# Moving three weight stages' conversion steps within the opening of an mLSTM and bilinear MoE kernel

## The chip, the cores and the metric

The kernel runs on one core of one Trainium2 chip. The metric is the device time of one execution in microseconds (us); the lower, the better. The core has TensorE (matrix products, PE in the profile, with its weight loads as PEld), VectorE (DVE), ScalarE (ACT), GpSimd (POOL) and SyncE (SP), which here issues the transfers between DRAM and the core's memory. Each engine works through its own instructions in order and waits for the others by semaphores.

## The reference

Two parts follow one another. The first is an mLSTM over 768 steps for 4 batches and 8 heads with a head dimension of 40; the second a bilinear layer with 1536 hidden units on all 3072 tokens, without a nonlinearity.

```python
for t in range(S):                                     # S = 768, for every batch and head
    m_new  = maximum(f_gate[t] + m, i_gate[t])
    f_stab = exp(f_gate[t] + m - m_new); i_stab = exp(i_gate[t] - m_new); m = m_new
    C = f_stab * C + i_stab * outer(v[t], k[t])        # 40 x 40 state
    n = f_stab * n + i_stab * k[t]
    y[t] = sigmoid(o_gate[t]) * (C @ q[t]) / maximum(abs(n @ q[t]), 1)
x   = y as [3072 tokens, 320]
out = ((x @ w_a) * (x @ w_b)) @ w_out                  # w_a, w_b: 320 x 1536; w_out: 1536 x 320
```

The weights arrive as 64-bit floats; everything else is 32 bits.

## The kernel before

**The mLSTM in chunks.** The sequence of each batch is cut into 6 chunks of 128 steps, so there are 24 chunks of work (n = 0 to 23, four batches to each position c). Within a chunk the recurrence becomes products of matrices: `begin_a` transposes q and k on TensorE (tile pT), `begin_e` makes the table of decays E, `begin_b` forms the scores pS and multiplies by E, `begin_c` multiplies by v (pV), `stage_u` updates the state (pU, from vw, which `weigh` makes on GpSimd), `stage_f` divides by the denominator and multiplies by the sigmoid of the output gate (the chunk's y, in tile osig), and `stage_d` transposes y on TensorE (pX) and splits it into a rounded part xh (ScalarE) and a remainder xl (VectorE). Later chunks use stages of the same names with operands of 16 bits in three parts, and pass the state through DRAM: `stage_u` rounds it into the tile cb (L648, L652, L655), writes it to c_dram (L658, L659) and reads it back (L661).

**The MoE in blocks.** The 24 chunks are grouped into 9 blocks of 2 or 3. For a block, `moe_block` runs over 12 slices of hidden units: `up` forms the products with w_a and w_b (pu, L812) from xh and xl, multiplies the two (g, L818 and L819) and splits the result (gh, gl); `down` multiplies by w_out into pd (L783).

**The weights in stages.** There are 32 weight stages; stages 0 to 7 serve the first three slices of hidden units: 0 to 3 are 128-row parts of w_a and w_b, 4 holds the last 64 rows of both, 5 to 7 are parts of w_out. Each stage is loaded as 64-bit words by `fetch` (L386, tile raw) and turned into a rounded 32-bit part and a remainder by four steps, each of which does its work once and calls the one it rests on:

- `signs(x)`: one Prelu on ScalarE (L414) takes sign and exponent from the upper words.
- `words(x)`: three operations on VectorE (L425, L426, L428) put the upper part together (tile cw) and the remainder from the lower words (tile cr).
- `leading(x)`: one rounding copy on ScalarE (L441).
- `rests(x)`: two products with plus and minus the identity on TensorE (pc, L451 and L452) and a sum on VectorE (L459) make the rounded-off remainder. For stage 4 the two 64-row halves are handled apart (L456 twice on ScalarE, L457 twice on VectorE).

`cw` and `cr` are rings of four places, `step` (written by signs) has four places too, and pc shares the three buffers of pu.

**The opening.** `start` (from L956 on) is written out by hand: `in_order` ties each engine's instructions into the order in which they stand in the text. It computes the first two chunks (n = 0 and 1), converts stages 0 to 4, and is left when both chunks' xh and xl and stage 4 are there, since the first `up` needs them. `busy(k)` issues k products of zeros (L961) that nothing reads; they occupy TensorE. `run(x, k)` advances a generator by k steps, or to its end; `run(d0, 1)` issues pX of chunk 0 and the next `run(d0)` its xh and xl. `gate_o(0, slice(0, 2))` is the sigmoid on the gates of the first two chunks (L218). The loads stand in the same function: SyncE issues them in the order q, k, weight stages, v, gates and so on, and `load(NS + 2)`, `fetch(18)`, `load(NS + 3)`, `fetch(26)` are the last ones there.

**Behind the opening.** The gates of the remaining steps are computed by `gates_rest`, again in order, which writes the decay table to DRAM (g_dram, L291); `load_g` reads a chunk's part back to all partitions (L225, tile gbc). The rest of the mLSTM, the MoE blocks and the conversion of the remaining stages are traced in one interleaved loop (the loop over kb at L1073); the order on each engine there comes from a planner, which simulates a timeline while it schedules the instructions.

Of the kernel before, what the change touches and what calls it, by code (L numbers as in the profile page):

```python
# [20 lines left out]
def kernel(  # L21
# [158 lines left out]
    def nat(n):  # L180
        return inner.get(n) or (qk[n % NQ], va[n % NQ])
# [33 lines left out]
    def gate_o(c, bs=slice(0, B)):  # L215
        hot[0] = 3
        x = osig[c][:, bs, 0:DM]
        nc.scalar.activation(x, x, AF.Sigmoid)  # L218
# [187 lines left out]
    def signs(x):  # L406
        if not turn(0, x):
            return
        raw, n = held[x]
        t = step[x % len(step)][:, :n]  # L410
        words = raw.bitcast(U32).rearrange("p (n w) -> p n w", w=2)
        held[x] += [t, words[:, :, 0]]
        with tc.issue_after(rounded[x - 2]) if x > 4 else nullcontext():
            nc.scalar.activation(  # L414
                t, words[:, :, 1].bitcast(F32), AF.Prelu, scale=2.0 ** -112, alpha=-(2.0 ** 32)
            )
# [16 lines left out]
    def leading(x):  # L433
        if not turn(2, x):
            return
        n, W, r = held[x]
        w = ws[x] = rpool.tile([P, 2, n], F32R, tag=f"s{x - 1}", name=f"w{x}")
        h = w[:, 0]
        if len(stages[x]) > 1:
            h = cpool.tile([P, WCH], F32R, tag="ct", name="ct", bufs=2)  # L440
        rounded[x] = nc.scalar.copy(h, W).ins  # L441
        held[x] += [w, h]
# [474 lines left out]
    def begin_c(n):  # L917
        c, b = chunks[n]
        s = st[n]
        if n >= NS:  # L920
            weigh(n)
        if n < NS:
            pV = ps_dn.tile([P, 512], F32, tag=f"pd{min(n, 2)}", name=f"pV{n}")
        else:
            pV = ps_at.tile([P, 512], F32, tag="pat", name=f"pV{n}")
        pv = pV[:, 0:H * DV].rearrange("p (h d) -> p h d", h=H)
        dense(n, pV, 3)
        for h in range(H):
            nc.tensor.matmul(pv[:, h], s["E"][:, h, :], nat(n)[1][:, h], start=True, stop=True)  # L929
            if h % HH == HH - 1:  # L930
                yield
        if c > 0:
            nc.vector.tensor_tensor(s["num"], pv, s["num"], op=ALU.add)
        else:
            s["num"] = pv
        yield
# [14 lines left out]
    with tc.tile_pool(name="spool", bufs=3) as spool:  # L951
# [4 lines left out]
        def start():  # L956
# [8 lines left out]
            def run(x, count=99):  # L965
                for _ in range(count):
                    if next(x, "end") == "end":
                        return
# [38 lines left out]
            rests(0)  # L1007
            run(b1)
            leading(1)
            gate_o(0, slice(0, 2))  # L1010
            rests(1)
            run(begin_c(0))
            weigh(0)
            signs(2)
            run(begin_c(1))
            run(stage_f(0))
            words(2)
            run(stage_u(0))
            load(NS + 2)
            weigh(1)  # L1020
            leading(2)
            signs(3)
            run(stage_f(1))
            d0, d1 = stage_d(0), stage_d(1)
            warm = ps_dn.tile([P, 512], F32, tag="pd2", name="warm2")
            busy(4)
            run(d0, 1)
            words(3)
            run(d0)
            leading(3)  # L1030
            busy(4)
            rests(2)
            signs(4)
            run(stage_u(1))
            fetch(18)
            load(NS + 3)
            fetch(26)
            busy(4)
            run(d1, 1)
            words(4)  # L1040
            run(d1)
            leading(4)
            busy(4)
            rests(3)
            busy(8)
            rests(4)
            signs(5)
            gate_o(0, slice(2, B))
# [71 lines left out]
```

## Time and profile before

| | us |
|---|---|
| three runs | 551.63, 552.08, 550.17 |
| median | 551.63 |
| the profiled execution | 551.88 |
| its span | 550.1 |
| TensorE busy | 537.8 (98%) |
| VectorE busy | 411.6 (75%) |
| ScalarE busy | 269.2 (49%) |
| GpSimd busy | 149.5 (27%) |

All times below are counted from the start of the span. Matmuls are pipelined, so TensorE's busy time includes time in which it does not work at its peak. A row of a timeline gives start, duration, engine, line, operation, what is written and read, a count, and, in square brackets, how long the engine had stood idle before and what ended that. A row of the chain of waits gives start, duration and what ran or was awaited. A row of the windows gives the stretch, its length, the busy time of TensorE, its weight loads, VectorE, ScalarE and GpSimd with the number of instructions, then the granted clock of TensorE (1.00 is full), the mean busy share of the 16 DMA engines and GB/s.

### The profile page before, as it was taken

To read this page: it belongs to the slowest core of one execution; us is meant where nothing else is said; L and a number is where in the kernel's file an instruction comes from. 1 tells how busy PE (TensorE), PEld (TensorE's weight loads), DVE (VectorE), ACT (ScalarE), POOL (GpSimd) and SP (SyncE) were. 2 spreads that over 40 slices of the span, in tenths; PEclk is the share of its full clock that TensorE was granted. 3 is DMA by queue.
4 is the path that set the end of the run, shared out by engine and by line. 5 is a ranking of instruction groups with operands and counts; after the bars stand their busy time and mean duration, and the time that the engine had idled before them with its cause. 6 is when DMAs were issued, how large, how long until landed. Compare 5 with 4: busy or idle time off the path is not lost.

```text
span 550.1 us, 11947 instructions
## 1 busy us (share of the span) xinstructions
PE 537.8 (98%) x4493; PEld 511.4 (93%) x4493; DVE 411.6 (75%) x906; ACT 269.2 (49%) x645; POOL 149.5 (27%) x224
## 2 busy tenths in 40 slices
PE   8999999899999999999999999999999899999997
PEld 5888888799999999999999999999999899999996
DVE  6889999977768785988868974988677846964332
ACT  5574488664425853645625664655354813321111
POOL 3102324545032340442233340444041203210000
PEclk9799999999999999999999999999999999999999
DMA  9999943284537665668646885758459403300001
GB/s 190 217 220 284 323 88 71 64 179 113 89 100 142 139 128 113 133 131 179 121 119 115 127 161 116 140 123 170 91 130 183 102 1 104 78 1 24 1 1 36
DMA packets 198549, 66.71 MB, mean 121 GB/s; under 512 B 184220, under 2 KB 191772, under 8 KB 198492
## 3 DMA queue, kind: packets, MB, share of 16 engines
q1 hardware_dynamic: 198444, 65.86, 56.6%
q8 instruction: 35, 0.57, 0.5%
q14 instruction: 22, 0.18, 0.1%
q10 hardware_dynamic: 48, 0.10, 0.0%
HBM read 41.11 MB, written 5.95 MB: 86 GB/s over the span
## 4 chain that ended last, share of the span: by engine, by line
PE 80%; DVE 6%; DMA 4%; ACT 4%; issue 2%; SPq 2%; POOL 0%; ACTq 0%; DVEq 0%; POOLq 0%
PE pu L812 42%; PE pd L783 20%; PE pU L630 3%; PE pV L603 3%; PE pS L544 3%; DMA T<-qks 2%; DMA osig<-in_o_gate_dram 1%; PE pX L709 1%; PE pV L929 1%; ACT gbc L492 1%; PE pI L570 1%; PE pS L886 1%; PE warm L961 1%; SPq L524 1%; PE pc L451 1%
## 5 line engine op out<-in xcount | busy, mean ns | idle before, releaser
L812 PE MATMUL pu<-xh,w 128*128 128x384 f32 (+1 forms) x1080 | 273.2, 322 | 1.5 <-DVE w L459 0.7
L812 PE MATMUL pu<-xl,w 128*128 128x384 f32 (+1 forms) x648 | 206.1, 320 | 0.0
L812 PEld LDWEIGHTS pu<-xh,w 128*128 128x128 f32 x1080 | 188.3, 188 | 4.0 <-DVE w L459 1.3
L783 PE MATMUL pd<-w,gh 128*128 128x320 f32 x576 | 127.2, 311 | 0.2 <-DVE gh L821 0.2
L812 PEld LDWEIGHTS pu<-xl,w 128*128 128x128 f32 x648 | 121.8, 188 | 0.0
L819 DVE TENSOR_TENSOR g<-pu,g 128x384 f32<-128x384 f32 (+1 forms) x108 | 54.4, 504 | 82.8 <-PE pu L812 47.6
L783 PEld LDWEIGHTS pd<-w,gh 128*128 128x128 f32 x576 | 96.3, 188 | 0.6 <-DVE gh L821 0.4
L818 ACT COPY g<-pu 128x384 f32<-128x384 f32 (+1 forms) x90 | 39.6, 440 | 103.3 <-PE pu L812 96.0
L783 PE MATMUL pd<-w,gl 128*128 128x320 f32 x288 | 84.7, 311 | 0.0
L614 POOL TENSOR_TENSOR num<-v,num 128x168 f32<-128x168 f32 x36 | 21.3, 593 | 210.3 <-DVE v L610 209.7
L823 DVE TENSOR_TENSOR gl<-g,gh 128x384 fp32r<-128x384 f32 (+1 forms) x92 | 57.3, 622 | 2.0
L492 ACT ACTIVATE gbc<-gbc,gtab 128x128 f32<-128x128 f32 x160 | 49.4, 390 | 12.3 <-POOL gbc L485 12.2
L783 PEld LDWEIGHTS pd<-w,gl 128*128 128x128 f32 x288 | 52.7, 188 | 0.2
L821 DVE CAST gh<-g 128x384 fp32r<-128x384 f32 (+1 forms) x108 | 42.2, 390 | 1.7
L515 ACT CAST qks<-r 128x320 bf16<-128x320 f32 x36 | 16.4, 458 | 30.1 <-DVE r L514 30.0
L610 DVE TENSOR_REDUCE v<-pV 128x168 f32<-128x504 f32 x36 | 24.1, 675 | 9.2 <-PE pV L603 9.1
L485 POOL TENSOR_SCALAR_AFFINE_SELECT gbc<-gbc 128x1024 f32<-128x1024 f32 x20 | 23.4, 1171 | 24.7 <-DMA gbc<-g_dram 23.3
L584 POOL TENSOR_TENSOR vw<-va,gtab 128x336 f32<-128x336 f32 x20 | 17.0, 852 | 47.5 <-PE pU L630 22.2
L553 DVE TENSOR_TENSOR gbc<-gbc,pb 128x512 f32<-128x512 f32 x36 | 25.4, 707 | 4.5 <-ACT pb L551 4.5
L520 ACT COPY qks<-qks 128x640 bf16<-128x640 bf16 x36 | 26.1, 725 | 0.7
L549 DVE TENSOR_TENSOR gbc<-pS,gbc 128x512 f32<-128x512 f32 x36 | 24.3, 679 | 1.7 <-PE pS L544 1.7
L551 ACT CAST pb<-gbc 128x512 bf16<-128x512 f32 x36 | 22.2, 617 | 5.7 <-DVE gbc L549 5.6
(152 smaller groups left out, 810.1 us busy)
## 6 DMA issues: line engine op xcount, KB each, us to landing
gbc<-g_dram SPq DMA_DIRECT2D x20, 512.0 KB
q<-in_q_dram SPq DMA_DIRECT2D x24, 160.0 KB
k<-in_k_dram SPq DMA_DIRECT2D x24, 160.0 KB
va<-in_v_dram SPq DMA_DIRECT2D x24, 160.0 KB
osig<-in_o_gate_dram SPq DMA_DIRECT2D x24, 160.0 KB
raw<-in_moe_w_out_dram SPq DMA_DIRECT2D x12, 320.0 KB
out_dram<-o SPq DMA_DIRECT2D x24, 160.0 KB
raw<-in_moe_w_a_dram SPq DMA_DIRECT2D x8, 384.0 KB
```

The lines of the kernel that those rows point to most:

```text
L485: nc.gpsimd.affine_select(E, E, pattern=[[0, H], [1, P]], compare_op=ALU.is_ge, fill=-1e30, base=0, channel_multiplier=-1,)
L492: nc.scalar.activation(E[:, h], E[:, h], AF.Exp, bias=beta[:, h:h + 1])
L520: nc.scalar.copy(qks[:, 0, :, lo:lo + 2 * D], qks[:, 1, :, D - lo:3 * D - lo])
L549: nc.vector.tensor_tensor(E, pS, E, op=ALU.mult)
L553: nc.vector.tensor_tensor(E, E, pb[:, 0], op=ALU.subtract)
L610: nc.vector.tensor_reduce(t, pv.rearrange("p h i d -> p h d i"), axis=mybir.AxisListType.X, op=ALU.add)
L783: nc.tensor.matmul(pd[t][:, 0:DM], a[:, cols], w, start=(ff == 0 and first), stop=(ff == NF - 1 and last),)
L812: nc.tensor.matmul(acc[j], a, r, start=(x == 0), stop=(x == len(terms) - 1),)
L818: (nc.vector.tensor_copy if ff in [1, 2] else nc.scalar.copy)(g, acc[0])
L819: nc.vector.tensor_tensor(g, acc[1], g, op=ALU.mult)
L821: nc.vector.tensor_copy(gh, g)
L823: (nc.gpsimd if kb * 12 + ff < 16 else nc.vector).tensor_tensor(gl, g, gh.bitcast(F32), op=ALU.subtract)
```

## The change

In `start` the steps of stages 2, 3 and 4 are put elsewhere among the chunks' steps. The signs of stage 2 stand in front of the sigmoid `gate_o` and its words between the two chunks' `begin_c`; its leading part and the signs of stage 3 stand ahead of the first chunk's y (`stage_f(0)`), the words of stage 3 right after it, and `rests(2)` in front of the first transpose. The second chunk's y (`stage_f(1)`) moves behind the first transpose, the leading part of stage 3 and the signs of stage 4; the words of stage 4 and `rests(3)` follow it. The second transpose stands ahead of a group of zero products and not behind it. One group of four and one group of eight zero products are gone, which the diff counts as twelve; the description of the change speaks of sixteen. The loads keep their order.

```diff
             run(b1)
             leading(1)
+            signs(2)
             gate_o(0, slice(0, 2))
             rests(1)
             run(begin_c(0))
             weigh(0)
-            signs(2)
+            words(2)
             run(begin_c(1))
+            leading(2)
+            signs(3)
             run(stage_f(0))
-            words(2)
+            words(3)
             run(stage_u(0))
             load(NS + 2)
             weigh(1)
-            leading(2)
-            signs(3)
-            run(stage_f(1))
+            rests(2)
             d0, d1 = stage_d(0), stage_d(1)
             warm = ps_dn.tile([P, 512], F32, tag="pd2", name="warm2")
-            busy(4)
             run(d0, 1)
-            words(3)
             run(d0)
             leading(3)
+            signs(4)
+            run(stage_f(1))
             busy(4)
-            rests(2)
-            signs(4)
+            words(4)
+            rests(3)
             run(stage_u(1))
             fetch(18)
             load(NS + 3)
             fetch(26)
+            run(d1, 1)
             busy(4)
-            run(d1, 1)
-            words(4)
+            leading(4)
             run(d1)
-            leading(4)
             busy(4)
-            rests(3)
-            busy(8)
             rests(4)
             signs(5)
             gate_o(0, slice(2, B))
```

## The prediction

> **What bounds the kernel now.** I read the page first, for the span and the load of the DMA engines.
>
> ```profile
> span 550.1 us, 11947 instructions
> ...
> DMA  9999943284537665668646885758459403300001
> ```
>
> The profiled execution took 551.88 us for its span of 550.1 us, so 1.78 us lie outside the span; the median of the three runs is 551.63, which is 0.25 us below the profiled one. A change in the span is subtracted from 551.88 and the result lowered by 0.25 to stand beside the median. The DMA row has its first five slices, up to about 69 us, at 9: the opening and the first MoE block lie under a saturated DMA.
>
> The second view is the chain of waits from 19 to 31 us, the stretch in which the change lies. Columns are start, duration and what ran.
>
> ```profile
> 19.49 1.47 PE pU L630 x16
> ...
> 22.20 0.64 PE pX L709 x3
> 22.84 1.12 PE warm L961 x4
> 23.96 0.32 PE pc L451
> 24.28 0.32 PE pc L452
> 24.60 1.16 PE pU L630 x16
> ...
> 26.43 0.33 PE pX L709 x3
> ...
> 27.68 1.16 PE warm L961 x8
> ```
>
> All of it is TensorE, in the order written out by hand: the first chunk's pU ends at 20.96, the first transpose pX waits behind four zero products until 22.20, the rounding products pc of stage 2 come at 23.96, the second pX at 26.43. The rows also show two speeds: three transposes take 0.64 us at 22.20 and 0.33 at 26.43. The windows say why (the number after the engines' busy times is the granted TensorE clock, then the DMA share):
>
> ```profile
> 18.44:19.00 0.56, 0.56 (x5) 0.56 (x4) 0.48 (x2) 0.24 (x1) 0.00 (x0) 0.50 1.52 141
> ...
> 25.26:25.35 0.09, 0.09 (x8) 0.09 (x6) 0.09 (x1) 0.00 (x0) 0.00 (x0) 0.96 1.10 400
> ```
>
> The clock is at half from 18.44 to 25.26.
>
> Third, VectorE's and ScalarE's rows of the same stretch.
>
> ```profile
> 17.30 0.17 DVE L671 TENSOR_SCALAR den<-pV 128x8 f32<-128x8 f32 x1 [0.36 <-PE pV L929]
> ...
> 18.52 0.49 DVE L682 TENSOR_TENSOR osig<-y,osig 128x320 f32<-128x320 f32 x1
> 18.93 0.35 DVE L425 TENSOR_SCALAR cw<-qks 128x384 uint32<-128x384 uint32 x1
> ...
> 19.71 0.56 DVE L428 SCALAR_TENSOR_TENSOR cr<-raw,qks 128x384 fp32r<-128x384 uint32 x1
> 20.19 0.16 DVE L671 TENSOR_SCALAR den<-pV 128x8 f32<-128x8 f32 x1
> ...
> 21.35 0.85 DVE L682 TENSOR_TENSOR osig<-y,osig 128x320 f32<-128x320 f32 x1
> ...
> 23.46 0.55 DVE L714 TENSOR_TENSOR xl<-pX,xh 128x384 fp32r<-128x384 f32 x1
> 24.63 0.56 DVE L459 TENSOR_TENSOR w<-pc,cw 128x384 fp32r<-128x384 f32 x1 [0.62 <-PE pc L452]
> ...
> 27.31 0.56 DVE L714 TENSOR_TENSOR xl<-pX,xh 128x384 fp32r<-128x384 f32 x1 [0.86 <-ACT xh L713]
> ...
> 29.66 1.14 DVE L457 TENSOR_TENSOR w<-pc,cw 64x384 fp32r<-64x384 f32 x2 [1.33 <-PE pc L452]
> ```
>
> ```profile
> 16.20 1.28 ACT L218 ACT_TABLE_LOAD   x1 [1.90 <-DMA osig<-in_o_gate_dram]
> ...
> 18.14 0.54 ACT L414 ACTIVATE qks<-raw 128x384 f32<-128x384 f32 x1
> ...
> 21.61 0.56 ACT L414 ACTIVATE qks<-raw 128x384 f32<-128x384 f32 x1
> 22.23 0.25 ACT L683 COPY osig<-osig 128x64 f32<-128x64 f32 x1
> ...
> 23.66 0.55 ACT L414 ACTIVATE qks<-raw 128x384 f32<-128x384 f32 x1
> ```
>
> VectorE is the engine that stands idle while TensorE works off its order: 0.62 us before 24.63, 0.86 before 27.31, 1.33 before 29.66. The opening's last weight step that the MoE needs, L457 of stage 4, ends at 29.66 + 1.14 = 30.80.
>
> Last, what follows the opening, by windows and then around the one long wait of the first block.
>
> ```profile
> 37.00:54.00 17.00, 17.00 (x147) 15.10 (x145) 16.90 (x44) 7.45 (x18) 3.73 (x5) 1.00 1.02 260
> ...
> 71.00:77.00 6.00, 5.83 (x46) 5.36 (x46) 6.00 (x16) 6.00 (x20) 1.17 (x2) 1.00 0.02 5
> 77.00:110.00 33.00, 30.98 (x232) 27.69 (x231) 32.36 (x82) 24.45 (x59) 14.20 (x20) 1.00 0.40 78
> ```
>
> ```profile
> 54.29 0.34 SPq L291 DMA_DIRECT2D g_dram<-va  x1
> ...
> 62.23 0.33 SPq L225 DMA_DIRECT2D gbc<-g_dram  x1
> 62.67 0.69 SPq L658 DMA_DIRECT2D c_dram<-cb  x2
> 63.90 0.68 SPq L659 DMA_DIRECT2D c_dram<-cb  x2
> ```
>
> ```profile
> SPq L225 <- DMA g_dram<-va: 3.3, 1, 3.3
> ```
>
> ```profile
> 63.20 0.76 POOL vw L584
> ...
> 64.24 3.65 DMA c_dram<-cb
> ```
>
> ```profile
> 68.04 0.33 ACT L648 CAST cb<-cst 128x168 bf16<-128x168 f32 x1 [3.81 <-DMA c_dram<-cb]
> ```
>
> ```profile
> 67.47 1.32 POOL L485 TENSOR_SCALAR_AFFINE_SELECT gbc<-gbc 128x1024 f32<-128x1024 f32 x1 [2.38 <-DMA gbc<-g_dram]
> ```
>
> ```profile
> 69.52 0.42 DVE L819 TENSOR_TENSOR g<-pu,g 128x256 f32<-128x256 f32 x1 [1.68 <-ACT g L818]
> ```
>
> From 37 to 54 us VectorE is busy 16.90 of 17 and from 77 to 110 us 32.36 of 33, so time that VectorE wins in the opening is worth as much up to the next meeting point. That point is at 62 to 69 us. SyncE waits 3.3 us at L225 until the gate table has been written to DRAM (issued at 54.29, landed when L225 goes at 62.23); only then do the state's writes L658 and L659 follow in its queue; the last of them lands at 64.24 + 3.65 = 67.89; ScalarE has sat for 3.81 us at L648, which needs that buffer, and all behind it on ScalarE (a leading part L441, signs L414, the copy g L818) waits too. VectorE then runs dry for 1.68 us. The gate table's read also ends late: GpSimd begins with it at 67.47.
>
> **The change part by part.** *Signs of stage 2 ahead of the sigmoid.* One Prelu of 0.54 us goes ahead of a ScalarE instruction that stood idle for 1.90 us until its gate landed (row 16.20). If the weights have landed by about 15.6, the idle time covers it and it costs nothing; without that cover it is 0.54 us on the sigmoid. The row at 18.14 has no idle time, so they landed by 18.14 at the latest; I take covered.
>
> *Words of stage 2 ahead of the first y.* The three VectorE operations run from 18.93 to 19.71 + 0.56 = 20.27, 1.34 us, and now stand in front of the y that ran from 17.30 to 18.52 + 0.49 = 19.01. So the first y ends about 1.3 us later, near 20.3, and with its copy of 0.25 us (row 22.23) near 20.6. Its reader pX cannot start before TensorE is through pU (20.96) and, now, the products pc of stage 2. That cover holds with 1.0 us to spare (21.60 below).
>
> *TensorE's order.* After pU come pc of stage 2 (0.32 + 0.32 at half clock, to 21.60), pX (0.64, to 22.24), four zero products (1.12, to 23.4), pc of stage 3 (0.64, to 24.0), pU of the second chunk (1.16, to 25.2). ScalarE's rounding and VectorE's xl follow pX by 23.46 - 22.84 = 0.62, so xl runs from 22.86 to 23.41. *The second y* then takes what it took from 20.19 to 21.35 + 0.85 = 22.20, 2.0 us, or the first one's 1.7: it ends at 25.1 to 25.4, with the copy at 25.4 to 25.7. So pX of the second chunk starts there against 26.43: 0.7 to 1.0 us won, and TensorE waits for it 0.2 to 0.5 us, a wait that the kernel before did not have; behind it stand only the zero products and pc of stage 4.
>
> *VectorE to the end of the opening.* Words of stage 4 (1.34), the difference of stage 3 (0.55), xl (0.56) and L457 of stage 4 (1.14) now run back to back: 25.1 to 25.4 + 3.6 = 28.7 to 29.0. The last pc does not hold them up: pX 0.33, eight zero products 1.16 (the row at 27.68), pc 0.35 give 27.5. Against 30.80 the opening ends **1.8 to 2.1 us earlier; I take 2.0**.
>
> *The zero products.* The diff drops one group of four and one of eight: twelve, where the description says sixteen. At full clock eight cost 1.16 us. The dropped ones lay on the chain, and their price is inside the 2.0, not beside it.
>
> *Bounds of the opening.* Signs of stages 3 and 4 move ahead of the y copies on ScalarE. The rows at 21.61 and 23.66 have no idle time, so the weights landed by then; signs of stage 4 come near 23.3 in the new order, which costs nothing that matters. Signs of stage 3 come near 18.7; had its weights landed only at 21.61, the first y copy would end at 21.61 + 0.54 + 0.25 = 22.4, pX 0.8 later than above, and the gain would be 1.2. I take about 2.0: 18.7 is 18.14, where ScalarE was through the sigmoid, plus a rounding of half a microsecond, and nothing on ScalarE waited for weights after the gate's wait that ended at 16.20. The leading parts (L441), moved with them, run on ScalarE in time that it has: its next use, the copy of the first y, does not come before 20.3; the copy of the second y stands behind the leading part of stage 3 and the signs of stage 4, which end near 23.9, 1.2 us before that y. The DMA issues keep their order on SyncE; nothing moves past another there.
>
> *What is late next.* In the rows of 62 to 69 us the DMA's dates do not move: its share is 1.02 from 37 to 54 us and it is full until the row 71 to 77 shows 0.02, so bytes that are issued in the same order land at the same time. L225 still goes at 62.23 and L658 at 62.67 to 63.36. The write L659 at 63.90 followed a GpSimd product (63.20 + 0.76) that would now be done 2 us sooner, so it can start at 63.36, 0.54 earlier. The gate table's read ends at 67.47 as before. ScalarE therefore comes to L648 two microseconds early and waits about 5.3 us instead of 3.81; VectorE's idle 1.68 becomes about 3.1. Of the 2.0 us, **between 0 and 0.6 come through; I take 0.5**, as the chain names that product as the releaser of the write.
>
> Sum: 551.88 - 0.5 = 551.4 in the profiled execution's own time, 551.1 beside the median.
>
> The Trainium skill, page "TensorE: Matmul & The Clock Gate", section "Part 1: The HAM clock gate (the "warmup" mystery)", says that the clock is halved after an idle activity window of about 3.4 us and restored after a busy one, and that the windows run free. The trace agrees: 25.26 - 18.44 = 6.82 us is two such windows. The rule speaks against taking zero products away; by it the gate could open later than in my sum, and that is the rival on the clock below.
>
> **The rivals.** *The gain is kept.* The order behind the opening is made by a planner that simulates time, and not by hand. If the table's write (54.29) goes out ahead of two of the weight loads, or other work is laid in front of L648, the meeting at 68 us moves along and all 2.0 us come through: 549.6 (549.0 to 550.4). For it: VectorE is full from 77 to 110 us, so nothing after the meeting gives the time back. Against it: table and loads that it competes with become ready by steps that all move earlier together.
>
> *The planner turns it to a loss.* L648 is placed further ahead on ScalarE, since the plan starts 2 us earlier, and the work that ran before 64.24 now stands behind a wait that ends at 67.9 whatever is done. Place: ScalarE at L648. Price: what is pushed behind the wait, at most the 2.0 us, then VectorE starts its full stretch with that much undone: 551.63 + 2.0 = 553.6. It decides once over half a microsecond of rounding work has changed sides, as that is all the nearer meeting gives. Against it: at 64.24 three short operations stood behind L648, and the plan put them there for reasons that move together.
>
> *The clock stays low.* If the lighter order leaves the gate shut until 25.26 + 3.41 = 28.67, the second pX and eight zero products take 0.64 + 2.32 instead of 0.33 + 1.16, L457 ends near 30.4, and 0.4 of the 2.0 is left; the meeting hides it: 551.4. One more 3.41 us, to 32.1, would cost the MoE's first 2.8 us 1.4 more, putting GpSimd's product at 63.20 some 1.2 later and the end at 552.9. For it: twelve zero products fewer. Against it: from 21.85 to 25.26 the same four zero products, pX and pc run as before, and more of pU.
>
> *The opening is no earlier.* A wait for weights that the rows do not show eats the 2.0: 551.6.
>
> **How the numbers follow.** Forecast (opening 2.0 earlier, 0 to 0.6 through): 0.48. Gain kept: 0.27. Planner's loss: 0.12. Clock: 0.08. No earlier: 0.05. What this kernel's measurement can tell from no change is about 0.3%, 1.65 us, so faster is below 549.98 and slower above 553.28. Faster: three quarters of the kept gain (0.20) and 0.05 of the forecast through a plan that differs a little, 0.25. Slower: more than half of the planner's loss and a fifth of the clock's, with 0.02 for the rest, 0.11. The range runs from 548.9, the kept gain's low end, to 553.3, short of the planner's full loss. The likeliest case alone spans 550.4 to 551.9.
>
> **What would show it.** Right: pc of stage 2 directly behind pU and the second pX near 25.5; L457 ending near 28.8; L225 again near 62.2 and ScalarE's wait at L648 over 5 us, ending near 67.5. The forecast is wrong if the wait at L648 ends before 66.5 or is gone, if the half clock lasts beyond 25.3, or if L225 goes before 61. A second y that ends after 26 would refute the walk through VectorE.

## The result and the profile after

The changed kernel takes 555.54 us (median of 13 runs, 552.45 to 560.42) against 552.08 us for the kernel before in the same comparison (median of 13). The ratio is **1.0072, with a 95% interval from 1.0044 to 1.0100**: slower, by 2.4 to 5.5 us. The prediction was 551.1 us, its range ended at 553.3, and it gave slower a chance of 0.11. It was wrong. Four of the 13 runs had a granted clock of 0.984 to 0.986 and took 559.1 to 560.4 us, the profiled execution (559.08) among them, and the other nine had 0.992 or more and took 552.5 to 557.7, with a median of 554.69 that is still 2.6 us above the kernel before.

The page of the changed kernel, its span and the granted clock of TensorE in 40 slices of 13.9 us:

```profile
span 557.3 us, 11927 instructions
...
PEclk9999996899999999999999999999999999999999
```

Half clock lay at 18.44 to 25.26 us before; that slice, the second, is full here. In its place the seventh and the eighth, 84 to 111 us, have 0.6 and 0.8.

The opening, in the timelines of TensorE, VectorE and ScalarE:

```profile
19.00 0.92 PE L630 MATMUL pU<-vw,k 128*64 128x42 f32 x16
19.86 0.45 PE L451 MATMUL pc<-cr,eye 128*128 128x384 f32 x1
...
24.26 0.52 PE L709 MATMUL pX<-ident,osig 128*128 128x128 f32 x3 [1.12 <-DVE osig L682]
```

```profile
27.08 0.56 DVE L714 TENSOR_TENSOR xl<-pX,xh 128x384 fp32r<-128x384 f32 x1
...
27.90 1.14 DVE L457 TENSOR_TENSOR w<-pc,cw 64x384 fp32r<-64x384 f32 x2
```

```profile
26.19 0.50 ACT L414 ACTIVATE qks<-raw 128x320 f32<-128x320 f32 x1 [1.18 <-DMA raw<-in_moe_w_out_dram]
26.59 0.46 ACT L713 CAST xh<-pX 128x384 fp32r<-128x384 f32 x1
```

The products pc of stage 2 follow pU directly, and L457 ends at 27.90 + 1.14 = 29.04, inside the 28.7 to 29.0 that were forecast to 0.04 us and 1.76 earlier than the 30.80 of before. The second pX comes at 24.26, not at 25.5, because this execution had the full clock in the opening. What it won there it lost again at a wait that the prediction did not have: the signs of stage 5 on ScalarE wait 1.18 us for a weight load, the second chunk's rounding xh stands behind them, and xl and L457 follow. In the text of `start` these signs come behind `run(d1)`, which issues xh, and behind `rests(4)`; ScalarE's order in this opening was therefore not that of the text, which the prediction walked through. Why is not known.

The meeting at 62 to 69 us, the rows that answer to those of before (SyncE's queue, ScalarE, GpSimd, VectorE):

```profile
61.48 0.33 SPq L225 DMA_DIRECT2D gbc<-g_dram  x1
```

```profile
67.80 0.33 ACT L648 CAST cb<-cst 128x168 bf16<-128x168 f32 x1 [2.18 <-DMA c_dram<-cb]
```

```profile
67.16 1.09 POOL L485 TENSOR_SCALAR_AFFINE_SELECT gbc<-gbc 128x1024 f32<-128x1024 f32 x1 [3.82 <-DMA gbc<-g_dram]
```

```profile
68.44 0.42 DVE L819 TENSOR_TENSOR g<-pu,g 128x256 f32<-128x256 f32 x1 [1.62 <-ACT g L818]
```

L225 goes 0.75 us earlier than before, the cast L648 0.24, GpSimd's gate table 0.31. The cast alone is inside the 0 to 0.6 us that the forecast let through. L648's wait did not grow to over 5 us, though: the new order has a leading part (L441) and signs (L414) in front of it that stood behind it before, so ScalarE came later. And more than the cast's 0.24 us comes past the meeting: the sum g, 69.52 before, starts 1.08 us earlier, and the 16 products pI that follow on TensorE start 1.46 us earlier, here in the kernel before and then in the changed one:

```profile
74.08 1.56 PE L906 MATMUL pI<-cst,T 40*128 40x42 f32 x16
```

```profile
72.62 1.56 PE L906 MATMUL pI<-cst,T 40*128 40x42 f32 x16
```

The loss comes behind that. The windows of the changed kernel over the first MoE block, with the clock third from the end:

```profile
78.00:84.40 6.40, 6.40 (x59) 6.17 (x56) 6.18 (x17) 5.12 (x9) 0.51 (x1) 1.00 0.72 109
84.40:87.80 3.40, 3.40 (x18) 3.38 (x17) 2.17 (x7) 2.60 (x6) 1.74 (x2) 0.53 0.73 194
87.80:91.40 3.60, 3.60 (x23) 2.71 (x21) 3.21 (x6) 3.59 (x11) 3.60 (x5) 0.97 0.02 5
91.40:101.60 10.20, 10.20 (x40) 9.27 (x40) 6.42 (x18) 3.65 (x10) 0.87 (x2) 0.50 0.00 0
```

The same two stretches in the kernel before:

```profile
84.40:87.80 3.40, 3.40 (x28) 3.23 (x28) 3.22 (x10) 3.36 (x7) 0.74 (x1) 1.00 0.56 161
...
91.40:101.60 10.20, 10.20 (x75) 9.43 (x74) 10.20 (x28) 6.28 (x18) 4.03 (x5) 1.00 0.11 32
```

From 91.40 to 101.60 TensorE finishes 40 products where it finished 75 before, and VectorE, which was full there, is busy for 6.42 us of 10.20. What stood ahead of the first half-speed stretch is in TensorE's timeline of the changed kernel:

```profile
81.25 1.88 PE L929 MATMUL pV<-va,gbc 128*128 128x42 f32 x16
83.05 1.16 PE L886 MATMUL pS<-T,T 40*128 40x128 f32 x8
```

These are small products, back to back, and TensorE is not idle. The kernel before has the same two groups and keeps its clock behind them:

```profile
82.77 1.87 PE L929 MATMUL pV<-va,gbc 128*128 128x42 f32 x16
84.57 1.16 PE L886 MATMUL pS<-T,T 40*128 40x128 f32 x8
```

That is one profile. A second execution of the same kernel (after_again, below) kept the full clock over this stretch and still had a span of 556.3. So I laid the profiles side by side by VectorE's 108 sums g (L819), which come in the same number in every kernel. The table gives how much later (+) a kernel starts the 1st, 7th, 13th, 31st, 37th, 43rd, 49th, 61st and 106th of them than the kernel before does; the heading has the time of that row in the kernel before.

```
                              37.3  84.9 118.0 188.7 218.7 248.0 280.4 342.0 534.2
after                         -2.8  -2.3  +5.1  +4.8  +6.3  +6.4  +6.8  +7.4  +7.2
after_again                   -2.3  -0.7  +1.5  +1.3  +2.7  +3.4  +5.3  +5.9  +6.2
late_old_order                -2.6  -2.9  -0.4  +0.8  +0.8  +0.9  +0.9  +1.3  +1.2
early_old_order               -1.6  -0.5  +1.7  +2.2  +3.6  +3.7  +5.2  +5.5  +5.1
old_opening_new_plan          -3.6  -3.0  -0.5  -0.1  +1.5  +1.3  +1.1  +1.4  +0.7
new_opening_old_plan          -1.7  +0.3  +0.7  +0.7  +0.7  +0.7  +0.3  +0.6  +0.6
new_opening_old_plan_two_cb   -1.5  -0.8  -0.1  -0.2  -0.2  -0.2  +0.3  +0.1  -0.1
fewer_zeros_old_plan          -3.4  +0.9  +2.0  +1.9  +2.0  +1.7  +3.7  +4.6  +4.2
fewer_zeros_two_cb            -2.9  -2.0  -0.4  -0.4  -0.4  -0.3  +0.8  +1.2  +0.7
after_more_zeros              -3.1  -1.9  -1.0  -1.4  +0.3  +0.1  -0.2  +0.1  -0.4
zeros_late_old_order          -2.5  -1.6  +5.7  +5.6  +5.7  +5.4  +5.9  +5.8  +5.9
before_dense6                 -1.6  -1.9  +0.2  +1.0  +1.0  +1.0  +2.3  +3.8  +4.4
before_two_cb                 -0.2  -1.3  -1.2  -1.2  -1.2  -1.2  -1.3  -0.9  -1.2
```

The 1st and the 106th of these rows, for the kernel before and then for the changed one (37.32 and 34.52, 534.18 and 541.37):

```profile
37.32 0.41 DVE L819 TENSOR_TENSOR g<-pu,g 128x256 f32<-128x256 f32 x1
...
534.18 0.56 DVE L819 TENSOR_TENSOR g<-pu,g 128x384 f32<-128x384 f32 x1 [2.54 <-PE pu L812]
```

```profile
34.52 0.41 DVE L819 TENSOR_TENSOR g<-pu,g 128x256 f32<-128x256 f32 x1
...
541.37 0.56 DVE L819 TENSOR_TENSOR g<-pu,g 128x384 f32<-128x384 f32 x1 [2.54 <-PE pu L812]
```

Each row is one execution, and the runs of one kernel spread over several microseconds, so a last column is not a kernel's loss. Read along a row, the table shows three things. Whatever a kernel has won by 37 us, at most 1.0 us of it is left at 118 us (before_two_cb, with 1.2, won nothing in the opening). Where it goes differs: with the order of the kernel before and one buffer cb little or none is left at 84.9 us, behind the meeting (+0.9 to -0.5; only before_dense6, with its added zero products, keeps more), while with the new order 0.7 to 3.0 us are still there and go between 84.9 and 118 us. The changed kernel loses 1.4 to 1.5 us between 189 and 219. And between 248 and 342 us kernels lose between nothing and 3 us. The experiments below take these apart.

### The profile page after: what moved, and what is told of

Read it like the earlier page. It is cut to its first block, busy times and chain, and to the rows that moved or that the text cites. A ratio compares the mean times of both kernels' runs of the same rounds, so it can differ in the third digit from the quotient of the medians.

```text
span 557.3 us, 11927 instructions
## 1 busy us (share of the span) xinstructions
PE 541.6 (97%) x4481; PEld 514.5 (92%) x4481; DVE 413.3 (74%) x906; ACT 268.8 (48%) x645; POOL 147.8 (27%) x224
## 4 chain that ended last, share of the span: by engine, by line
PE 72%; DVE 9%; DMA 9%; issue 4%; ACT 2%; SPq 2%; POOL 1%; ACTq 0%; DVEq 0%; POOLq 0%
PE pu L812 39%; PE pd L783 18%; PE pV L603 3%; PE pS L544 2%; DMA T<-qks 2%; PE pU L630 2%; DMA osig<-in_o_gate_dram 2%; PE pX L709 1%; DMA raw<-in_moe_w_b_dram 1%; DMA raw<-in_moe_w_out_dram 1%; DMA c_dram<-cb 1%; PE pI L570 1%; PE pS L886 1%; PE pV L929 1%; DVE gbc L549 1%
## 5 line engine op out<-in xcount | busy, mean ns | idle before, releaser
L812 PE MATMUL pu<-xl,w 128*128 128x384 f32 (+1 forms) x648 | 208.3, 323 | 0.0
L812 PEld LDWEIGHTS pu<-xh,w 128*128 128x128 f32 x1080 | 190.7, 190 | 4.0 <-ACT gbc L850 1.3
L812 PEld LDWEIGHTS pu<-xl,w 128*128 128x128 f32 x648 | 123.5, 191 | 0.1
L819 DVE TENSOR_TENSOR g<-pu,g 128x384 f32<-128x384 f32 (+1 forms) x108 | 54.6, 505 | 85.6 <-PE pu L812 50.9
L823 DVE TENSOR_TENSOR gl<-g,gh 128x384 fp32r<-128x384 f32 (+1 forms) x92 | 53.0, 576 | 2.0
L821 DVE CAST gh<-g 128x384 fp32r<-128x384 f32 (+1 forms) x108 | 43.4, 401 | 1.6
L792 ACT COPY o<-pd 128x320 f32<-128x320 f32 x24 | 8.7, 431 | 34.5 <-PE pd L783 34.5
```

Source lines behind the costliest of these rows:

```text
L812: nc.tensor.matmul(acc[j], a, r, start=(x == 0), stop=(x == len(terms) - 1),)
L819: nc.vector.tensor_tensor(g, acc[1], g, op=ALU.mult)
L821: nc.vector.tensor_copy(gh, g)
L823: (nc.gpsimd if kb * 12 + ff < 16 else nc.vector).tensor_tensor(gl, g, gh.bitcast(F32), op=ALU.subtract)
```

## Experiments

The order of the instructions behind the opening is made by the planner, and with the change it differs on all engines: on TensorE up to the 1434th of 4048 instructions behind the opening, about 219 us, and not after. To separate the edit in the opening from this new order, a kernel was given either order outright: each engine's instructions behind the opening are tied into a recorded list, "old plan" being that of the kernel before, "new plan" that of the changed one.

```diff
+    for e, runs in ORDER.items():
+        line = [mine[e][x] for first, n in runs for x in range(first, first + n)]
+        for x, y in zip(line, line[1:]):
+            tc.add_manual_dep(y, x.name, ...)
```

All kernels below compute the whole result. Except in after_again, which is the changed kernel itself, their line numbers are shifted by 3 (two_cb and the orders) or 8 (dense6) against the kernel before.

### The opening alone, the order alone

> The changed opening, and behind it every engine's instructions held in the order that the planner made for the kernel before. If the planner's new order is what costs (theory plan), the loss is gone: -1 to +0.5 us against the kernel before. If the twelve dropped zero products cost through the clock, wherever the clock falls (theory zeros), the loss stays: +3 to +4 us. If the order within the opening itself costs (theory opening), it stays too, and the next kernels tell the two apart.

> The opening of the kernel before, and behind it the order that the planner made for the changed kernel. Theory plan: slower by 3 to 5 us. Theories zeros and opening: as the kernel before, -0.5 to +0.5 us.

Measured: the new opening with the old plan 1.0023 [0.9998, 1.0048]; the old opening with the new plan 1.0020 [0.9991, 1.0049]. Neither alone is the loss of 1.0072, and the two together, 1.0043, fall short of it, though within the intervals.

The meeting in the first of them (ScalarE, then VectorE):

```profile
67.62 0.33 ACT L651 CAST cb<-cst 128x168 bf16<-128x168 f32 x1 [4.93 <-DMA c_dram<-cb]
```

```profile
69.09 0.42 DVE L822 TENSOR_TENSOR g<-pu,g 128x256 f32<-128x256 f32 x1 [2.79 <-ACT g L821]
```

With the order held fixed, this is close to the forecast: a wait of about 5.3 us was expected and is 4.93, ending near 67.5 (67.62), VectorE idle for about 3.1 (2.79). The opening's gain is lost there. What the forecast lacked is what the idle time does next; TensorE and the windows of the same kernel:

```profile
69.11 0.44 PE L454 MATMUL pc<-cr,eye 128*128 128x384 f32 x1 [1.90 <-ACT g L821]
```

```profile
66.00:70.00 4.00, 2.10 (x14) 1.85 (x14) 1.21 (x5) 2.38 (x8) 1.30 (x2) 0.99 0.99 265
70.00:73.40 3.40, 3.40 (x18) 3.40 (x17) 3.40 (x6) 3.40 (x12) 2.47 (x3) 0.51 0.24 48
```

TensorE stands still for 1.90 us, is busy for 2.10 of 4 us, and then has half its clock for 3.4 us. The gain of 1.7 us is not only lost: at 84.9 us the kernel is 0.3 us late (table).

The second kernel has the **old** opening in an execution with the full clock, and its L457 shows how far the gain of 1.76 us was one of the edit:

```profile
18.00:28.00 10.00, 9.75 (x98) 7.92 (x98) 8.70 (x22) 7.57 (x19) 1.81 (x2) 1.00 1.16 207
```

```profile
27.06 1.14 DVE L460 TENSOR_TENSOR w<-pc,cw 64x384 fp32r<-64x384 f32 x2 [0.83 <-PE pc L455]
```

At full clock the old opening ends at 28.20, **0.84 us earlier than the new one** at full clock (29.04). At half clock from 18 to 25 us it ended at 30.80, and the new one, in new_opening_old_plan, at 28.20 + 1.14 = 29.34:

```profile
18.40:25.30 6.90, 6.90 (x48) 5.74 (x48) 5.22 (x15) 2.74 (x8) 0.75 (x1) 0.52 1.06 203
```

```profile
28.20 1.14 DVE L460 TENSOR_TENSOR w<-pc,cw 64x384 fp32r<-64x384 f32 x2
```

The edit wins 1.5 us in an execution whose opening is throttled for some 6.8 us and loses 0.8 in one whose opening is not. The other profiles agree: the old opening with its zero products ends at 30.63 us in before_two_cb (half clock from 18.5 to 25.3) and at 29.22 in before_dense6 (19.2 to 22.6), while the new opening without the twelve ends between 29.04 and 29.90 whatever its clock.

### The zero products

> The kernel before with its own order on every engine, less the twelve zero products that the change drops (the group of four ahead of the first transpose and the group of eight ahead of the last stage's rounding). Theory zeros: slower by 2 to 4 us, with a lower mean clock in more of its runs. Theory plan: the opening gets up to 1 us shorter and the wait at L648 takes that back, so -0.5 to +0.5 us.

> The changed opening with the twelve zero products put back at the same two places, the old order behind it. Theory zeros: 2 to 4 us faster than the same kernel without them. Theory plan: within 0.5 us of the same kernel without them, and within 0.5 us of the kernel before.

> The changed kernel, own order throughout, with the twelve zero products put back into the opening (four in front of the first chunk's y, eight in front of the rests of stage 4). Theory that taking them away costs time here (2.7 us in the kernel before, by its own run): 1 to 2.7 us less than the changed kernel, 1.002 to 1.005. Rival, that they cost and bring nothing because the won time is lost at the meeting at 68 us either way: the same as the changed kernel, 1.006 to 1.008; the opening then ends 1 to 1.7 us later than 29.04 and ScalarE's or GpSimd's wait at 67 us is shorter by as much.

The edit of the first, and the reverse of it for the other two:

```diff
             warm = ps_dn.tile([P, 512], F32, tag="pd2", name="warm2")
-            busy(4)
             run(d0, 1)
...
             rests(3)
-            busy(8)
             rests(4)
```

Measured: the kernel before without the twelve 1.0057 [1.0028, 1.0086]; the new opening with the twelve, old plan, 1.0014 [0.9991, 1.0037] (without them 1.0023); the changed kernel with the twelve **1.0019 [0.9992, 1.0047]**, against 1.0072 and, in its repeat, 1.0075. So twelve products of zeros are worth about 3 us in the kernel before and in the changed kernel, and nothing that can be told with the new opening and the old plan. In the kernel before without them the end of the opening and the meeting show why (VectorE, ScalarE, TensorE, windows):

```profile
26.25 1.14 DVE L460 TENSOR_TENSOR w<-pc,cw 64x384 fp32r<-64x384 f32 x2
```

```profile
68.06 0.33 ACT L651 CAST cb<-cst 128x168 bf16<-128x168 f32 x1 [7.27 <-DMA c_dram<-cb]
```

```profile
69.56 0.69 PE L454 MATMUL pc<-cr,eye 128*128 128x384 f32 x1 [4.25 <-ACT g L821]
```

```profile
63.50:66.90 3.40, 1.81 (x14) 1.43 (x12) 0.90 (x3) 0.00 (x0) 0.37 (x1) 1.00 0.79 224
66.90:74.30 7.40, 4.74 (x20) 4.74 (x21) 4.76 (x12) 6.24 (x21) 3.30 (x4) 0.54 0.42 113
...
66.90:67.50 0.60, 0.00 (x0) 0.00 (x0) 0.00 (x0) 0.00 (x0) 0.60 (x1) 0.99 0.76 241
67.50:74.30 6.80, 4.74 (x20) 4.74 (x21) 4.76 (x12) 6.24 (x21) 2.70 (x4) 0.50 0.39 101
```

The opening ends at 27.39, 3.4 us earlier than in the profile of before and 0.8 earlier than the old opening at full clock, the wait at the cast ends where it ends in the others, at 68.06, and the whole of the gain is idle time. TensorE stands still for 4.25 us, from 65.31 to 69.56, and has half speed for 6.8 us: it sets in at 67.5, 2.2 us into the wait, and lasts for 4.7 us of work behind it.

### The wait at the cast taken away

> The opening of the changed kernel, with the order behind it that the kernel before has, and the buffer cb of the state's rounded copy doubled, so that ScalarE's cast at 68 us no longer waits for the write of the copy before. Theory that the 1.8 us won in the opening are lost at that wait (4.93 us in the same kernel with one buffer) and turn into an idle stretch of TensorE that trips the clock: the wait at the cast is gone, VectorE's idle 2.79 us at 69 falls below 1, no half speed at 70 to 73, and the kernel comes out 1 to 2.5 us faster than with one buffer (about 554.2): 551.5 to 553, which is as fast as the kernel before or faster. Rival, that another date of the same DMA queue (the gate table's read, which GpSimd begins with at 67 us) ends the stretch whatever ScalarE does: the idle time moves to the instruction behind GpSimd's table, and the time stays within 0.7 us of the kernel with one buffer.

> The kernel before without the twelve zero products, its own order behind the opening, and the buffer cb doubled, so that ScalarE's cast at 68 us (7.27 us of waiting in the same kernel with one buffer) needs no earlier write. Theory that the 2.7 us this kernel loses with one buffer come from TensorE's idle time of 4.25 us at 69 us, which halves its clock from 67 to 74: the idle time shrinks to that of GpSimd's gate table (some 2 us), no half speed there, and the time is 1 to 2.7 us less than with one buffer (1.0057): 1.000 to 1.004. Rival (the loss is a later date of the DMA, of which the write into cb is not one): 1.005 to 1.007 again, with the loss between the 42nd and the 48th g product at 248 to 284 us.

> The changed kernel with the buffer cb doubled, own order. Theory that idle time at the meeting near 68 us (ScalarE 2.18 and 3.17 us at the cast in the two profiles of the changed kernel) is what the loss grows from: 1 to 3 us less than the changed kernel, 1.002 to 1.005, as the doubled buffer brought the kernel before without the twelve zero products from 1.0057 to 1.0003. Rival (in the changed kernel the idle time there is short, 0.2 to 1.2 us on TensorE, and the loss lies elsewhere): 1.006 to 1.008.

> The kernel before with the buffer cb doubled and nothing else. Theory that ScalarE's wait of 3.81 us at the cast is what bounds the stretch to 69 us: the wait goes, GpSimd's gate table (2.38 us of waiting at 67 us) bounds it next, 0 to 0.7 us are won, 0.9985 to 1.000. Rival (any shift of the dates moves later waits on the DMA by chance, and the doubled buffer helped only where the idle time at the meeting tripped the clock): 1.000 to 1.004.

```diff
-        cb = apool.tile([P, 3, HH, DV], BF16, tag="cb", name=f"cb{n}", bufs=1)
+        cb = apool.tile([P, 3, HH, DV], BF16, tag="cb", name=f"cb{n}", bufs=2)
```

Measured: fewer zeros **1.0003 [0.9979, 1.0028]** (1.0057 with one buffer); new opening with the old plan 1.0006 [0.9978, 1.0035] (1.0023); kernel before 0.9995 [0.9964, 1.0026]; changed kernel 1.0101 [1.0066, 1.0136] (1.0072). With the old plan the doubled buffer gives back what the missing zero products cost: idle time at the meeting and the clock after it were their price there. ScalarE and the windows of the fewer-zeros kernel with two buffers:

```profile
67.63 2.45 ACT L495 ACTIVATE gbc<-gbc,gtab 128x128 f32<-128x128 f32 x8 [3.67 <-POOL gbc L488]
```

```profile
63.50:66.90 3.40, 3.40 (x25) 3.08 (x25) 3.37 (x11) 0.46 (x2) 0.39 (x1) 1.00 1.01 341
66.90:74.30 7.40, 5.99 (x46) 5.22 (x46) 4.76 (x11) 6.67 (x22) 3.18 (x4) 1.00 0.39 99
```

The next date of the same queue, the gate table's read, now holds ScalarE for 3.67 us, but TensorE has work meanwhile and keeps its clock: from 66.90 to 74.30 us it finishes 46 products where it finished 20 with one buffer. The gain of the opening still does not arrive at the end: 2.9 us at 37, 0.4 at 118. In the changed kernel, whose wait at the cast is short, the doubled buffer does not help (1.0101, higher than either theory had it), so there the price of the zero products is not seen to be paid at this place.

### Which stretch of the new order

> The changed kernel with its own order of instructions up to about 167 us (the first 1010 of TensorE's 4048 behind the opening, 285 of VectorE's 848, 220 of ScalarE's 600) and from there on the order of the kernel before. Theory of two losses in the order (the new order loses some 1.5 us by 118 us, in the stretch of 42-column products, and 1.3 us again at 188 to 220 us, where ScalarE waits 6.0 us for the output copy against 3.1): the second loss is gone, 1 to 2 us less than the changed kernel, 1.003 to 1.006 of the kernel before, and the step of VectorE's 37th g product stands no further behind the kernel before than its 31st does. Rival (the order behind 167 us costs nothing, the loss is the clock and the DMA's dates alone): the same as the changed kernel, 1.007.

> The opening of the changed kernel, the order of the kernel before up to about 167 us, and from there on the order of the changed kernel. Theory of two losses: the stretch of 42-column products at 90 to 118 us is as in the kernel before, no half speed there, and only the loss at 188 to 220 us is left: 1.003 to 1.005. Rival (order behind 167 us costs nothing): 1.001 to 1.003, as with the order of before throughout (1.0023).

The recorded lists were cut where both orders have the same instructions in front, at about 167 us (TensorE's 1010th, VectorE's 285th, ScalarE's 220th, GpSimd's 82nd, SyncE's 104th).

Measured: the changed kernel with the old order behind the cut 1.0052 [1.0022, 1.0083]; with the old order in front of the cut 1.0034 [1.0005, 1.0064]. The waits of ScalarE between 188 and 222 us, in the kernel before, after_again, late_old_order and early_old_order:

```profile
ACT o L792 <- PE pd L783: 3.1, 1, 3.1
```

```profile
ACT o L792 <- PE pd L783: 6.0, 1, 6.0
```

```profile
ACT o L795 <- PE pd L786: 3.3, 1, 3.3
```

```profile
ACT o L795 <- PE pd L786: 6.0, 1, 6.0
```

ScalarE's copy of the third block's output stands further ahead in the new order and waits 6.0 us for it. The table says what the new order does there: between 189 and 219 us every kernel with the new order there loses 1.4 to 1.8 us (after +1.5, after_again +1.4, early_old_order +1.4, old_opening_new_plan +1.6, after_more_zeros +1.7), and every kernel with the old order there 0.0 to 0.1 (late_old_order, zeros_late_old_order, new_opening_old_plan, fewer zeros). In the timed ratios it is smaller than their intervals: 0.0020 between the changed kernel and late_old_order. That the copy is the cause is argued from its wait; it was not moved by itself.

### More work in the thin stretch

> The changed kernel once more with the order of its instructions behind the opening written out (the order it has by itself), to stand on one chip beside the next three. Every theory expects the result of the change again: 1.005 to 1.009 times the kernel before, some 3 us. The theory of the clock adds that its time goes with the time that TensorE is given half speed between 60 and 130 us, which the profile shows for this one execution: with some 15 us at half speed the time is 558 to 560, with 7 us or less 552 to 555.

> The changed kernel, same order behind the opening, with 24 more zero products on TensorE, in three-packs in front of the transposed products of chunks 4 and 5 (they lie at about 50 to 110 us and are 24 x 0.14 = 3.4 us of TensorE work that computes nothing). Theory of the clock (the loss of the change is TensorE being given half speed for windows of 3.4 us between 66 and 102 us, because too few columns run through it there): the thin stretch is filled, the half speed of 84 to 102 us goes away or shrinks to one or two windows, and the kernel comes out 1 to 3 us faster than the changed kernel in spite of the added work, 552 to 554, and its heavy executions of 559 to 560 are gone. Theory of the planned order (the loss is the new order itself, engines waiting in another sequence, and the clock only follows): the added work costs 0 to 3 us more than the changed kernel, 555 to 558.

> The kernel before with the same 24 zero products and the order behind the opening that it has by itself. It shows what the zero products cost where the profile shows no half speed in that stretch: theory of the clock, 0 to 1 us more than the kernel before (552 to 553.5), or up to 1 us less if some executions of the kernel before are throttled there too; theory of the planned order, the same cost as in the changed kernel, 0 to 3 us.

```diff
     def dense(n, bank, count):
-        if NS <= n < NE:
+        if NS <= n < 6:
```

Measured: the changed kernel again 1.0075 [1.0046, 1.0103]; with 24 more zero products 1.0069 [1.0046, 1.0092]; the kernel before with them 1.0071 [1.0048, 1.0094]. Where the clock was not in question the 24 products cost 0.0071, 3.9 us, a little more than the 3.5 us that they last (eight took 1.16 in the opening); in the changed kernel they cost nothing. The forecast gain of 1 to 3 us from the clock theory did not come; that no run would take 559 to 560 us any more did (558.13 at most), in six runs. The profile of after_again is the stronger answer. Its windows:

```profile
84.40:87.80 3.40, 3.40 (x28) 3.23 (x28) 2.71 (x8) 3.00 (x6) 0.74 (x1) 1.00 0.41 157
87.80:91.40 3.60, 3.60 (x25) 2.84 (x23) 3.60 (x9) 3.44 (x8) 2.75 (x4) 1.00 0.25 50
91.40:101.60 10.20, 10.20 (x75) 9.60 (x75) 10.20 (x30) 6.50 (x18) 3.62 (x4) 1.00 0.07 16
```

The same program as the changed kernel, the same stretch, 75 products instead of 40 and the full clock. Half speed there is a matter of the single execution. It costs some 5 us when it comes (from 84.9 to 118 us the one profile loses 7.4 us and the other 2.2), and the theory that it alone is the loss falls: without it the kernel ends at +6.2 in the table. The order may make it likelier: ten microseconds at half speed near 91 to 102 us are in three of the eleven profiles with the new order there and in none of the nine with the old, which is too few to show it.

### Which zero products, and whether the losses add up

> The changed kernel with four of the twelve zero products put back, those in front of the first chunk's y. Theory that they matter for the clock of the opening (more work there opens the gate earlier): most of the 3 us come back, 1.002 to 1.004, and the eight alone bring nothing. Theory that it is the end of the opening that counts: nothing comes back, 1.006 to 1.008.

> The changed kernel with eight of the twelve zero products put back, those in front of the rests of stage 4 at the end of the opening. Theory that it is the clock of the opening: 1.005 to 1.008. Theory that the eight keep TensorE from running dry at the meeting or change the date of what follows the opening: 1.002 to 1.004. If both kernels come out between, at 1.004 to 1.006, the two groups add up and no single place decides.

> The opening of the changed kernel with the twelve zero products put back, the changed kernel's order up to about 167 us and the order of the kernel before from there on. Theory that the losses add up (3 us for the zero products, 1.4 us for the order at 188 to 220 us, nothing else): 1.0019 less 1.4 of 553, that is 0.9985 to 1.0015, as fast as the kernel before or faster. Rival (the order behind 167 us costs nothing in the time, only in one profile): 1.002 again.

> The opening of the changed kernel with the twelve zero products put back, the changed kernel's order up to about 167 us, the order of the kernel before from there on, and the buffer cb doubled. Theory that the doubled buffer helps only with the old order in front of 167 us: no better than the same kernel with one buffer (1.0017), 1.001 to 1.006. Rival (it takes the idle time at 68 us away in any order): 0.998 to 1.001.

Measured: four of the twelve 1.0074 [1.0056, 1.0093]; eight 1.0063 [1.0046, 1.0080]; twelve and the old order behind 167 us 1.0017 [0.9992, 1.0042]; the last with two buffers 1.0008 [0.9976, 1.0040]. Neither group alone brings the 3 us back; only both together do (1.0019). I expected one of them to decide, or the two to add up to something halfway. The old order behind 167 us brought nothing measurable on top of the twelve (1.0017 for 1.0019), against 1.4 us expected, and the doubled buffer's 1.0008 does not tell its two theories apart. And the profile of zeros_late_old_order has half speed at the same place as the changed kernel, zero products or not:

```profile
84.40:87.80 3.40, 3.40 (x19) 3.28 (x18) 2.76 (x9) 2.52 (x7) 1.01 (x1) 0.62 0.69 204
...
91.40:102.00 10.60, 10.60 (x44) 9.62 (x45) 6.79 (x18) 4.44 (x12) 1.62 (x3) 0.53 0.00 0
```

No version beats the kernel before by more than its interval; before_two_cb comes nearest, with 0.9995 and a profile that is 1.2 us ahead from 118 us on.

## Why the prediction was wrong

**The opening, 1.8 to 2.1 us earlier.** The date was right (29.04 for 28.7 to 29.0), but by luck, as two errors cancelled. The step "TensorE's order" was worked out at half clock; at the full clock that the changed kernel's profile had, the second pX came 1.2 us sooner, and "Bounds of the opening", which asked for late weights at the signs of stages 2, 3 and 4, missed those of stage 5: ScalarE waited 1.18 us there with xh queued behind. And the gain of 2.0 itself was a difference to an execution with a throttled opening; against an unthrottled one (28.20) the new opening is 0.84 late.

**What is late next.** This step held only for the old order. There the wait at the cast became 4.93 us and ended at 67.62, and nearly nothing came through. In the changed kernel it failed: the wait was 2.18 us, not over 5, and 1.1 to 1.5 us came past the meeting, to be lost behind it. The step also took the idle time to cost nothing. With the old order TensorE's idle time at the meeting went with half speed for 3.4 us (new_opening_old_plan) or 6.8 (fewer zeros), and doubling cb, which removes the idle time, removed the loss in the latter (1.0057 to 1.0003).

**The zero products, "their price is inside the 2.0".** This is the step that failed by most. Their work is on the chain of the opening, so I took leaving them out as pure gain. Put back into the changed kernel they bring its ratio from 1.0072 to 1.0019: a term that the sum put at a gain was a loss of some 3 us. I looked for their effect on the clock in the opening alone and gave it 0.08. In the kernel before without them it came at 67.5 to 74.3 us, at the wait that the won time had become; in the changed kernel neither profile has half speed there, and how they act in it is open (below). The Trainium skill, page "TensorE: Matmul & The Clock Gate", section "HAM oscillation — how this bites in real kernels", describes a wait for a transfer that crosses a window of more than some 3.4 us and a cold start behind it. The traces agree only in part: the wait of 4.25 us had half speed from 2.2 us after its start, and in new_opening_old_plan 1.90 us of standing still were followed by 3.4 us at half speed.

**The rival of the planner.** The side was right, the place was not. I put it at L648 and priced it at the 2.0 us won. The new order eased that wait (2.18 us) and lost 1.4 to 1.8 us at 189 to 219 us, where a copy on ScalarE waits 6.0 us instead of 3.1. The order was said to be made by a planner, yet the sum counted every instruction behind 69 us as unmoved: it had one term there, 0.5 us kept, and none for a loss.

**Where the 4 us go.** Shown: the opening's gain is all but spent by 118 us in every profile; the order at 189 to 219 us costs 1.4 to 1.8 us in every profile that has it, of which the times with the twelve products put back show nothing at the end (1.0017 for 1.0019); ten microseconds of half speed at 84 to 102 us cost some 5 us in the executions that have them. Not settled: how twelve zero products give back 3 us in the changed kernel, where the opening ends at 29.04 without and 29.23 us with them. The mean of (1 - clock) times the time falls from 4.8 to 2.6 us per run with them, but the kernel before has 4.2 in the same comparison and is no slower, so the clock is no more than a part. Another part may lie at 248 to 280 us, where ScalarE waits for the o gates' load. In the kernel before and in after_again:

```profile
255.47 1.28 ACT L218 ACT_TABLE_LOAD   x1 [4.96 <-DMA osig<-in_o_gate_dram]
```

```profile
259.83 1.28 ACT L218 ACT_TABLE_LOAD   x1 [5.97 <-DMA osig<-in_o_gate_dram]
```

Issued at 249.02 and 252.28 us, the load lands 6.45 and 7.55 us later. In nineteen profiles the load took 5.6 to 7.0 us in the eleven whose step from 248 to 280 us lost at most 0.5, and 7.0 to 7.8 in the other eight, of which seven lost 1.1 to 2.0. The six with the twelve products and no others are all at 6.4 to 6.7; those without them lie on both sides. What decides the landing was not tried.

## What to carry to other kernels

A gain in front of a date that is set by a transfer can be worse than lost: with the old order it became idle time on TensorE just ahead of the date, and 1.9 to 4.3 us of that went with 3.4 to 6.8 us at half speed, so cover for TensorE is best counted where the gain will be spent and not where it is won. When a planner orders what follows, hold its order fixed in one experiment and exchange it in another before anything is ascribed to the edit, and compare the edited stretch in executions with the same clock, since an opening that is throttled in one profile and not in the other makes up a gain of 2.6 us (30.80 against 28.20) by itself.

## What was unexpected in the hardware

Half speed came without TensorE being idle: from 81.25 to 84.21 us the changed kernel issues 24 small products back to back, and from 84.4 to 87.8 it has a clock of 0.53. The section of the Trainium skill named above gives the rule as no idle gap of more than some 3.4 us, and here there was no gap. The same two groups lie in the kernel before (82.77 to 85.73) with the full clock behind them. They last 2.96 us, and the half speed of these profiles comes in lengths of about 3.4, 6.8 and 10.3 us; so whether one such window holds little else seems to depend on where the windows fall in that execution. This was argued from the profiles and not tried by itself.

Twenty-four zero products, spread over 59 to 98 us, cost the kernel before 3.9 us, and its profile shows more of the loss later than there: from 37 to 118 us it loses 1.8 us, from 219 to 534 us 3.4 (table). Why it comes so late stays open.
